# The first pair of heads: k transposed into two PSUM banks and copied in two halves, its rest first, and shorter first products of ones

## The chip, the cores and the metric

The kernel runs on one core of one Trainium2 chip. The metric is the device time of one execution in microseconds. Before the change it is 775.11 us, the median of three runs (774.7 to 775.67). Five engines work side by side: TensorE (PE, matmuls, with its weight loads shown as PEld), VectorE (DVE), ScalarE (ACT), GpSimd (POOL) and SyncE (SP, which issues most DMA transfers).

## The reference

Attention that keeps, for each query, only the scores not below the 32nd largest, followed by a feed-forward block with a squared ReLU:

```python
# q, k, v: (8, 8, 576, 64) float32 (batch, heads, sequence, head_dim)
scores = (1 / sqrt(64)) * q @ k^T
kth = the 32nd largest score of each row
scores = where(scores >= kth, scores, -1e9)
attn = softmax(scores)                       # over the row
x = (attn @ v), heads side by side           # (4608, 512)
h = maximum(x @ w_in, 0)                     # w_in (512, 2048)
out = (h * h) @ w_out                        # w_out (2048, 512), float32 out
```

## The kernel before

The work is cut into pairs of heads (four pairs for each of eight batches). Of each pair, q, k and v are loaded as rows (tiles rq, rk, rv), q and k are turned by PE into the tile qk (head dimension on the partitions), and v is copied to bf16 (vb). Queries are worked on in groups of 128 of both heads; the last 64 queries of two pairs together make a fifth group. For one group PE computes the scores of both heads into three PSUM banks (`score`), ACT copies them to SBUF (L755), DVE folds the 576 scores of each row into shorter lists of maxima (L905), POOL makes the lists of the minima (L900), and DVE finds the 32nd largest by rounds of MAX8 and MATCH_REPLACE8 (L934 to L946). ACT then makes a mask (L965), PE turns the scores and adds the mask in PSUM (`attend`), ACT takes the exponential (L1021), and PE multiplies by v. The results of two pairs are normalised, transposed, and fed to the feed-forward products (`feed`) in chunks of up to 256 rows.

No order of the instructions is written by hand. Every piece of work is recorded with `pl.op(engine, duration, priority, function, ...)`, with the tiles that it reads, writes, takes from a pool and releases. `Plan.schedule` (in the class Plan) then plays the whole program with these durations: each engine takes the ready piece with the lowest priority number whose tiles can be had. A piece with `nbf` isn't ready before that time from the start. A piece counts as ended after its duration plus a tail for its engine (TAIL: 0.165 us for PE, 0.12 for ACT, 0.084 for DVE) and 0.035 us, and only then is a tile's slot free. `Emitter` writes the engines' instructions in the order so found and puts in the semaphore waits, between instructions of one engine too. So a changed duration or piece anywhere can change the order of all that comes later.

PSUM has eight banks in three pools: `ps_s` (three banks, the scores), `ps_e` (three banks, the turned scores of `attend`), both with one slot that is handed out in the order in which the tiles were made, and `psum` (two single banks, for everything else, to whoever asks first).

For the first pair, three functions stand apart. `load_first` issues the transfers of rk (half from ACT's queue, which also loads its rest, the last 64 rows of both heads; half from SP's), of the first 128 rows of q (rq), and then of the other q rows (rq2). `first_pair` has PE transpose the first block of q into the tile tx (`o_x`), four blocks of k into the tile tk (`o_k`), and then the rest of k into columns 128 to 192 of tx. ACT copies q's 128 columns (L638) and the rest twice (L641) from tx, DVE copies k's 512 columns from tk in one instruction (L639). The score of group 0 needs all of these copies. The other blocks of q follow behind it (`later`).

PE has nothing to do until the first data lands. `setup` gives it products of a matrix of ones meanwhile, each of 512 columns into a tile of `psum` that nobody reads. They have the highest priority number (1e5) and are marked `fill`: such a piece is dropped when its turn comes more than 0.3 us after its `nbf`, and later ones also when PE has been busy enough. All wait for `lit`, the writing of the ones by DVE. The first ones have `nbf` 0, 0.43, 0.86 and so on up to 3.87 us and a duration of 0.43; later ones follow from 8 us on. In the profile all matmuls stand under the helpers' lines: L582 is `mm`, L585 is `tr`, a transpose.

## Time and profile before

| | |
|---|---|
| median of three runs | 775.11 us |
| the profiled execution | 774.41 us, its span 772.6 us |
| mean granted TensorE clock | 0.998 |
| instructions | 27813 |
| busy: PE, DVE, ACT, POOL | 713.3, 751.6, 717.9, 687.6 us |
| DMA | 52.63 MB, mean 68 GB/s |

The span runs from the first to the last instruction; what the execution takes beyond it lies around the program. A row of the timeline has the start, the duration, the engine, the line, the operation, the tile written and the tile read, the shapes, the count, and in brackets how long the engine had been idle before and what ended that. A row of a group has the count, then the busy time in total and the mean duration of one in ns, and then the idle time before them. The table of windows gives for each stretch the busy time of each engine with its number of instructions, the granted clock, the DMA engines' share and GB/s.

### The profile page before, as it was taken

The numbers are of one execution on the slowest core, as the hardware profiler recorded it, in microseconds if no ns is written. First come the engines' busy times: TensorE is split into PE (matmuls) and PEld (weight loads), VectorE is DVE, ScalarE is ACT, GpSimd is POOL, SyncE is SP. The second block draws the span as 40 slices with busy tenths as digits, with TensorE's granted clock in tenths as the row PEclk, the third lists the DMA queues.
The fourth block names the chain that finished last, engine by engine and source line by source line (L and its number), as shares of the span: only waits on it lengthen the run. The fifth ranks groups of instructions, "written<-read, shape, count | busy, mean of one in ns | idle before, by whom it ended". The sixth has DMA issues, their size and how long they took to land.

```text
span 772.6 us, 27813 instructions
## 1 busy us (share of the span) xinstructions
PE 713.3 (92%) x10680; PEld 528.2 (68%) x10680; DVE 751.6 (97%) x3589; ACT 717.9 (93%) x1141; POOL 687.6 (89%) x720
## 2 busy tenths in 40 slices
PE   7888888999989999998999889999899999999999
PEld 3656666666666676666767657686677777767776
DVE  5999999999999999999999999899999999999996
ACT  4799989899899999999999999999999999998884
POOL 4898998889789899989999899899999998989991
PEclk9999999999999999999999999999999999999999
DMA  7657452032400134103340043301332021100101
GB/s 191 182 137 196 132 135 52 23 83 48 114 11 9 51 83 95 32 16 85 70 99 10 18 111 86 69 6 46 93 82 67 11 68 38 34 23 23 36 23 34
DMA packets 145033, 52.63 MB, mean 68 GB/s; under 512 B 137088, under 2 KB 137344, under 8 KB 144896
## 3 DMA queue, kind: packets, MB, share of 16 engines
q1 hardware_dynamic: 144224, 50.66, 26.7%
q8 instruction: 84, 1.38, 0.8%
q14 instruction: 53, 0.43, 0.2%
q10 hardware_dynamic: 672, 0.16, 0.1%
HBM read 36.70 MB, written 9.44 MB: 60 GB/s over the span
## 4 chain that ended last, share of the span: by engine, by line
ACT 58%; PE 31%; DVE 8%; issue 2%; DVEq 0%; ACTq 0%
PE ps L582 26%; ACT w L965 13%; ACT p L1021 12%; ACT s L755 12%; ACT g L1140 7%; PE ps L585 5%; ACT hz L776 4%; ACT g L1155 3%; DVE f L943 2%; DVE f L905 2%; ACT o L1172 2%; DVE c L939 2%; ACT av L1087 2%; ACT qk L711 1%; ACT qk L712 1%
## 5 line engine op out<-in xcount | busy, mean ns | idle before, releaser
L900 POOL TENSOR_TENSOR f<-u,f 128x864 int32<-128x864 int32 x138 | 236.7, 1715 | 7.6
L965 ACT ACTIVATE w<-s,kth 128x576 bf16<-128x576 f32 x278 | 220.2, 829 | 3.5 <-DVE kth L946 3.5
L943 DVE MATCH_REPLACE8 f<-c,f 128x98 f32<-128x98 f32 (+2 forms) x840 | 221.2, 270 | 0.0
L939 DVE MAX8 c<-f 128x8 f32<-128x98 f32 (+2 forms) x840 | 201.5, 272 | 0.0
L582 PE MATMUL ps<-qk 64*128 64x384 f32 (+3 forms) x1280 | 179.5, 427 | 6.9 <-DVE f L905 5.8
L900 POOL TENSOR_TENSOR u<-f,s 128x576 int32<-128x576 int32 x138 | 166.5, 1206 | 16.6 <-DVE f L905 15.9
L1021 ACT ACTIVATE p<-ps 128x1152 bf16<-128x1152 f32 x144 | 169.1, 1174 | 12.5 <-PE ps L582 11.9
L755 ACT COPY s<-ps 128x1152 f32<-128x1152 f32 x140 | 162.0, 1157 | 17.3 <-PE ps L582 16.9
L582 PEld LDWEIGHTS ps<-qk 64*128 64x128 f32 (+1 forms) x1280 | 130.5, 175 | 39.6 <-DVE f L905 11.8
L582 PE MATMUL ps<-wo,g 128*128 128x512 bf16 (+1 forms) x592 | 142.9, 375 | 2.7 <-ACT qk L714 1.2
L582 PE MATMUL ps<-xt,win 128*128 128x256 bf16 (+1 forms) x1280 | 132.5, 252 | 8.5 <-ACT g L1140 3.6
L900 POOL TENSOR_TENSOR u<-s 128x288 int32<-128x288 int32 x138 | 110.2, 799 | 29.8 <-ACT s L755 26.5
L905 DVE TENSOR_TENSOR f<-ps,f 128x288 f32<-128x288 f32 x280 | 123.7, 442 | 0.1
L946 DVE MAX8 kth<-f 128x8 f32<-128x296 f32 x280 | 120.7, 456 | 0.0
L585 PEld LDWEIGHTS ps<-ident,s 64*128 64x128 f32 x2520 | 96.8, 139 | 30.9 <-ACT w L965 15.1
L582 PEld LDWEIGHTS ps<-xt,win 128*128 128x128 bf16 x1280 | 97.2, 98 | 29.3 <-ACT g L1140 6.0
L934 DVE MAX8 f<-f 128x8 f32<-128x288 f32 x280 | 114.7, 447 | 0.0
L585 PE MATMUL ps<-ident,s 64*128 64x64 f32 x2520 | 107.0, 227 | 4.6 <-ACT w L965 4.1
L1152 POOL TENSOR_TENSOR g<-g 128x512 bf16<-128x512 bf16 x86 | 89.4, 1042 | 2.9 <-ACT g L1140 2.6
L582 PEld LDWEIGHTS ps<-wo,g 128*128 128x128 bf16 x592 | 49.6, 98 | 55.2 <-issue 5.7
L1140 ACT ACTIVATE g<-ps 128x512 bf16<-128x512 f32 x140 | 86.2, 641 | 1.0 <-PE ps L582 0.9
L582 PEld LDWEIGHTS ps<-vb,p 128*128 128x128 bf16 (+1 forms) x1600 | 54.0, 100 | 32.7 <-ACT g L1140 10.5
(104 smaller groups left out, 859.1 us busy)
## 6 DMA issues: line engine op xcount, KB each, us to landing
rv<-in_v_dram SPq DMA_DIRECT2D x64, 128.0 KB, 2.4
rk<-in_k_dram SPq DMA_DIRECT2D x63, 128.0 KB, 2.5
rq<-in_q_dram SPq DMA_DIRECT2D x62, 128.0 KB, 2.5
out_dram<-o SPq DMA_DIRECT2D x31, 256.0 KB, 2.2
g<-in_moe_w_in_dram SPq DMA_DIRECT2D x8, 512.0 KB, 4.2
g<-in_moe_w_out_dram SPq DMA_DIRECT2D x8, 512.0 KB, 4.3
out_dram<-o SPq DMA_DIRECT2D x10, 128.0 KB, 2.3
rq<-in_q_dram SPq DMA_DIRECT2D x32, 32.0 KB, 2.5
```

The costliest lines, as they stand in the source:

```text
L582: return pe.matmul(o, l, r, start=start, stop=stop, skip_group_check=True)
L585: return pe.matmul(o, i, ident, is_transpose=True, skip_group_check=True, **kw)
L755: cp = [pl.op("act", 1.1, tg - LEAD + 1, lambda: act.copy(at(st)[:, :, 0:S], two(banks(ss)[:, FIRST_AT:], SECOND, S)), r=[ss], w=[st])]
L900: return pl.op("gp", dur, prio, lambda: gp.tensor_tensor(o().bitcast(I32), x().bitcast(I32), y().bitcast(I32), op), **kw)
L905: return dve(.36, lambda: vec.tensor_tensor(o(), two(banks(ss)[:, FIRST_AT + c:], SECOND, QUART), x(), ALU.max), r=[ss], **kw)
L934: prev[i] = [dve(.065 + HALF / 960, lambda i=i: vec.max(at(f)[:, i, A + 7:A - 1:-1], at(f)[:, i, M + QUART:E]), after=prev[i] + [low], hol ...
L939: lambda i=i, t=t, c0=c0, c1=c1: vec.max(eighth(t, i), at(f)[:, i, c0:c1]),
L943: lambda i=i, t=t, c0=c0, c1=c1: vec.match_replace(at(f)[:, i, c0:c1], eighth(t, i), at(f)[:, i, c0:c1], NEG), hold=[f])]
L946: ks.append(chain(kth, i, prev[i], .065 + (8 + HALF) / 960, lambda i=i: vec.max(eighth(kth, i), at(f)[:, i, A:M + QUART]), hold=[f]))
L965: masks[i:] = [pl.op("act", .77, tw + .8 * i, lambda i=i: act.activation(at(wt)[:, i, :], at(st)[:, i, 0:S], ACTF.Relu, bias=kth[:, i, n:n ...
L1021: return act.activation(at(pt)[:, :, :].rearrange("p c (h q) -> p h c q", h=2), bass.AP(x.tensor, x.offset, [x.ap[0], [APART, 2], [64, 9], ...
L1140: return act.activation(at(g)[:, 0:kf * nt], bank(hh)[:, 0:kf * nt], ACTF.Relu)
```

## The change

`first_pair` gets a fourth tile, tk2, from the pool `ps_e`. The rest of k is now transposed right after q's block (`o_r`) and ahead of the k blocks. Of these, blocks 0 and 1 go into tk and blocks 2 and 3 into tk2, and DVE copies each tile with an instruction of 256 columns. In `setup`, the list of the first products of ones keeps seven with a duration of 0.43 us; eleven with a duration of 0.11 us, 0.11 us apart from 3.01 us on, take the place of the other three, and a product with a duration under 0.2 us has 128 columns in place of 512.

```diff
         def first_pair(rq, rq2, rk, rv, qk, vb, base):
-            tk, tx, tq = Tile(psum), Tile(psum), Tile(psum)
+            tk, tx, tq, tk2 = Tile(psum), Tile(psum), Tile(psum), Tile(ps_e)
...
             o_x = pl.op("pe", .15, base - 45.2, flips(tx, rq, [0]), r=[rq], w=[tx], take=[tx, qk])
-            o_k = pl.op("pe", .5, base - 45.1, flips(tk, rk, [0, 1, 2, 3]), r=[rk], w=[tk], take=[tk], order=[o_x])
-            pl.op("pe", .2, base - 45, lambda: tr(bank(tx)[:, 128:192], at(rk)[0:64, 4, :, :].rearrange("p h d -> p (h d)"),
-                                                  ident32[0:64, 0:64]), r=[rk], w=[tx], order=[o_k])
+            o_r = pl.op("pe", .2, base - 45.15, lambda: tr(bank(tx)[:, 128:192], at(rk)[0:64, 4, :, :].rearrange("p h d -> p (h d)"),
+                                                  ident32[0:64, 0:64]), r=[rk], w=[tx], order=[o_x])
+            o_k = pl.op("pe", .25, base - 45.1, flips(tk, rk, [0, 1]), r=[rk], w=[tk], take=[tk], order=[o_r])
+            pl.op("pe", .25, base - 45, flips(tk2, rk, [2, 3]), r=[rk], w=[tk2], take=[tk2], order=[o_k])
             pl.op("act", .3, base - 42.5, lambda: act.copy(at(qk)[:, 0:128], bank(tx)[:, 0:128]), r=[tx], w=[qk])
-            pl.op("dve", .6, base - 42.5, lambda: vec.tensor_copy(at(qk)[:, 640:1152], bank(tk)), r=[tk], w=[qk])
+            for i, t in enumerate((tk, tk2)):
+                pl.op("dve", .3, base - 42.5 + .01 * i, lambda i=i, t=t: vec.tensor_copy(
+                    at(qk)[:, 640 + 256 * i:896 + 256 * i], bank(t)[:, 0:256]), r=[t], w=[qk])
...
-        times = [(COLD * i, COLD) for i in range(int(WARM / COLD)) if COLD * i < 4.2]
+        times = [(COLD * i, COLD) for i in range(7)] + [(3.01 + .11 * i, .11) for i in range(11)]
...
         for x, dur in times:
             t = Tile(psum)
-            pl.op("pe", dur, 1e5, lambda t=t: mm(bank(t), ones_bf[:, :], ones_bf[:, :].unsqueeze(1).broadcast_to(
-                [P, 4, P]), True), w=[t], take=[t], after=[lit], nbf=x, fill=True)
+            pl.op("pe", dur, 1e5, lambda t=t, n_=1 if dur < .2 else 4: mm(bank(t)[:, 0:P * n_], ones_bf[:, :], ones_bf[:, :].unsqueeze(1).broadcast_to(
+                [P, n_, P]), True), w=[t], take=[t], after=[lit], nbf=x, fill=True)
```

## The prediction

> **What bounds the kernel now.** I read the page's busy shares first, then a table of windows, then what VectorE (DVE) waits for, and last the timeline of the first 9 us, because everything that the diff names lies there.

> ```profile
> span 772.6 us, 27813 instructions
> PE 713.3 (92%) x10680; PEld 528.2 (68%) x10680; DVE 751.6 (97%) x3589; ACT 717.9 (93%) x1141; POOL 687.6 (89%) x720
> ```

> ```profile
> core 0: us, PE busy (x) PEld busy (x) DVE busy (x) ACT busy (x) POOL busy (x), PEclk, DMA share, GB/s
> 0.00:9.00 9.00, 7.20 (x30) 3.22 (x30) 0.96 (x3) 3.04 (x6) 6.16 (x43) 1.00 0.58 131
> 9.00:30.00 21.00, 17.04 (x150) 11.00 (x149) 20.74 (x92) 14.21 (x22) 9.94 (x12) 0.92 0.80 200
> 30.00:100.00 70.00, 58.94 (x932) 45.05 (x934) 69.93 (x337) 65.84 (x100) 65.33 (x59) 1.00 0.61 159
> 100.00:200.00 100.00, 92.45 (x1369) 65.82 (x1365) 99.75 (x481) 89.80 (x135) 88.45 (x78) 1.00 0.29 70
> 200.00:300.00 100.00, 92.10 (x1353) 68.51 (x1352) 99.14 (x476) 98.05 (x160) 91.28 (x98) 1.00 0.23 54
> 300.00:400.00 100.00, 91.93 (x1394) 67.56 (x1395) 99.71 (x476) 99.83 (x164) 93.37 (x100) 1.00 0.26 63
> 400.00:500.00 100.00, 93.67 (x1467) 70.06 (x1462) 97.48 (x467) 99.49 (x164) 92.35 (x101) 1.00 0.26 58
> 500.00:600.00 100.00, 94.78 (x1420) 72.18 (x1419) 98.75 (x473) 98.64 (x164) 94.44 (x100) 1.00 0.25 60
> 600.00:700.00 100.00, 95.97 (x1503) 72.61 (x1500) 99.58 (x485) 92.99 (x148) 89.99 (x83) 1.00 0.14 37
> 700.00:760.00 60.00, 58.12 (x967) 44.20 (x968) 58.96 (x290) 51.87 (x80) 55.74 (x52) 1.00 0.08 22
> 760.00:772.60 12.60, 11.06 (x122) 8.00 (x121) 6.60 (x24) 4.19 (x9) 0.52 (x1) 1.00 0.14 47
> ```

> ```profile
> DVE qk L639 <- PE ps L585: 4.6, 1, 4.6
> DVE f L905 <- ACT s L755: 3.5, 5, 2.6
> DVE f L943 <- POOL f L900: 2.8, 2, 1.9
> ```

> DVE is the bound. It loses 8.0 us in the first 9 us, 6.0 us in the last 12.6, and in the 751 us between only 7.0 us (0.26 + 0.07 + 0.25 + 0.86 + 0.29 + 2.52 + 1.25 + 0.42 + 1.04). So whatever the first pair gains or loses before DVE's first fold is passed on to the end nearly whole, and whatever a new order of the middle does is seen as a change of those 7.0 us. The waits (engine, line and releaser; then total, times, longest) say that 2.8 of the 7.0 come from two waits for POOL's fold.

> **The first 9 us.** These are rows of the timeline (start, duration, engine); some come from narrower windows, so that single instructions stand alone.

> ```profile
> 1.06 3.81 PE L582 MATMUL ps<-ones_bf 128*128 128x512 bf16 x10 [1.06 <-DVE ones_bf L1328]
> 1.27 0.49 SPq L609 DMA_DIRECT2D rq<-in_q_dram  x1
> 1.29 0.71 ACTq L609 DMA_DIRECT2D rk<-in_k_dram  x1
> 3.43 0.10 PEld L582 LDWEIGHTS ps<-ones_bf 128*128 128x128 bf16 x1 [0.32 <-PE ps L582]
> 3.86 0.10 PEld L582 LDWEIGHTS ps<-ones_bf 128*128 128x128 bf16 x1 [0.33 <-PE ps L582]
> 4.26 0.10 PEld L582 LDWEIGHTS ps<-ones_bf 128*128 128x128 bf16 x1 [0.30 <-PE ps L582]
> 4.48 0.10 PEld L582 LDWEIGHTS ps<-ones_bf 128*128 128x128 bf16 x1
> 4.49 0.38 PE L582 MATMUL ps<-ones_bf 128*128 128x512 bf16 x1
> 4.71 0.14 PEld L585 LDWEIGHTS ps<-ident,rq 128*128 128x128 f32 x1
> 4.93 0.86 PE L585 MATMUL ps<-ident,rk 128*128 128x128 f32 x5
> 5.21 0.14 PEld L585 LDWEIGHTS ps<-ident,rk 128*128 128x128 f32 x1
> 5.52 0.14 PEld L585 LDWEIGHTS ps<-ident,rk 64*128 64x128 f32 x1 [0.17 <-issue]
> 5.63 0.69 DVE L639 COPY qk<-ps 128x512 f32<-128x512 f32 x1 [4.62 <-PE ps L585]
> 5.83 0.27 ACT L638 COPY qk<-ps 128x128 f32<-128x128 f32 x1 [2.52 <-PE ps L585]
> 5.99 0.34 ACT L641 COPY qk<-ps 128x64 f32<-128x64 f32 x2
> 6.43 0.97 PEld L582 LDWEIGHTS ps<-qk 64*128 64x128 f32 x8 [0.78 <-ACT qk L641]
> 8.11 0.14 PEld L585 LDWEIGHTS ps<-ident,rq 64*128 64x128 f32 x1 [0.17 <-issue]
> 8.32 0.09 PEld L582 LDWEIGHTS ps<-ones_bf 128*128 128x128 bf16 x1
> ```

> The first score (6.43) waits for two chains that end together: DVE's copy of k (to 6.32) and ACT's three copies (to 6.33). The flips ahead of them are not held by data but by the products of ones, whose PSUM slots they take over. The last product runs from 4.49 to 4.87, and the first k flip, which takes its slot, comes 0.06 later at 4.93; the q flip at 4.71 takes the slot of the product before. The data was there, by these rows of the DMA view (KB, then us from issue to landing):

> ```profile
> rq<-in_q_dram SPq DMA_DIRECT2D x1, 64.0 KB, 2.8
> rk<-in_k_dram ACTq DMA_DIRECT2D x1, 32.0 KB, 3.3
> ```

> q landed at 1.27 + 2.8 = 4.07, the last of k at 1.29 + 3.3 = 4.59.

> **The change, part by part.** Durations of the nearest shapes:

> ```profile
> L582 PE MATMUL ps<-ident_bf 128*128 128x128 bf16 x81 | 7.5, 222 | 7.6 <-ACT p L1021 7.5
> L905 DVE TENSOR_TENSOR f<-ps,f 128x288 f32<-128x288 f32 x280 | 123.7, 442 | 0.1
> L918 DVE TENSOR_TENSOR f<-f,s 128x576 f32<-128x576 f32 x2 | 1.5, 748 | 0.0
> ```

> *Short products.* The first seven long ones stay, and 11 of 0.11 us replace the last three. By the planner's rules a short one holds one of two slots for 0.11 + 0.165 + 0.035 = 0.31 us, and a filler over 0.3 us late is dropped. Followed by hand: numbers 1, 4, 7 and 10 (from 0) are dropped and seven are issued, two per 0.31 us. On the chip the same two slots set the pace: each waits for the end of the product two before it. The first two shorts load at 3.86 and 4.26, where long ones 8 and 9 loaded, since they wait for the same products. From there two take 0.222 + 0.06 = 0.28 us, so numbers 4 and 6 load at about 4.54 and 4.82, and the sixth ends at 5.04. The q flip takes the sixth's slot: 5.10 in place of 4.71. Less is streamed, but the end comes 0.39 us later. The bounds are 4.65 if the flips wait for data alone (landing plus 0.06), and 5.28 if the shorts run at half clock (0.05 us more each).

> *Rest first.* The 64-row weight load doesn't overlap: 0.31 us after the last 128-row load (5.21 to 5.52), and the next 128-row load is 0.21 us behind it (8.11 to 8.32). So rest loads at 5.41, and the first k flip at 5.62. ACT's copies start when rest is done, at about 5.72, and take the same 0.50 us (5.83 to 6.33): 6.22. This chain is 0.11 us earlier than before and no longer ends last; its cover is 0.7 us of the DVE chain below.

> *Two copies.* From first k load to DVE's start is 0.70 us for four flips (4.93 to 5.63), 0.49 us for two at 0.105 us a flip. A copy of 256 columns, by the slope between 288 and 576 columns (1.06 ns a column), is 442 - 34 = 0.41 us, so two take 0.82 us, against 0.69 for one. The first copy starts at 5.62 + 0.49 = 6.11 and ends at 6.52; k's second half is ready at 6.32, so the second copy goes on to 6.93. Before, it was 6.32. The start is thus 0.61 us later. With the flips bound by data alone, rest at 4.65 gives copies from 5.35 to 6.17, a gain of 0.15 us; with the late bound of the shorts the loss is 0.8 us. I take +0.6, because the slot rule is seen twice in the rows (4.65 to 4.71, 4.87 to 4.93). The second bank itself costs nothing: it is taken from the pool of three banks that the first attention product uses only after the first top-k. The fourth PE instruction moves a dependence on POOL's set-up to the second score, where set-up has long ended.

> *The order of the rest.* The planner believes in another start than the chip: by its own durations the last copy is over at 6.46 before and 6.27 now (from its zero), so its first score is 0.19 us earlier. All later work is planned from there against release times that stay absolute (weights, fillers, the MoE products), with two PSUM slots in free order. I expect the written order of every engine to differ in many places. The work itself is the same, so DVE's busy time stays, and only the 7.0 us of gaps are drawn anew. How far they can move is read from the windows: 100 us lose between 0.25 and 2.52 us, mean 0.93, spread 0.86, so 7.5 such stretches spread by 2.4 us. The gaps can't fall below zero but can grow freely; I add 0.3 us for that.

> Sum: 774.41 (the profiled execution: 772.6 of span and 1.8 around it) + 0.6 + 0.3 = 775.3. The median of the three runs is 0.7 above that execution, so **776.0** on its scale. Bounds on the sum: start -0.15 to +0.8, order -2.8 (both POOL waits gone) to +4.8 (two standard spreads).

> [...] The weight loads of the ones are 0.43 apart up to 3.86, and 0.22 apart at 4.26 and 4.48: the array doubled its pace at about 4.2 (and the mean granted clock of 0.92 from 9 to 30 us says that it was lowered once more).

> [...]

> **Rivals.**
> 1. *Order worse, slower.* One more wait of DVE for POOL's fold at L943, or another stretch like 400 to 500 us. Price 2.5 us (that stretch's loss), total 775.1 + 0.6 + 2.5 = 778.2. For it: POOL is 89% busy, and ACT 98% to 99.8% from 200 to 600, so a fold planned late has little room to catch up. It decides from 1.0 us of added gaps.
> 2. *Order better, faster.* Both POOL waits go: -2.8 + 0.6, 772.9. Against it: such waits are rare already, and they must go without others coming.
> 3. *Cold start.* Half clock through the first score: four flips +0.3, the score's 0.97 us of loads and their products up to +1.2: 775.1 + 0.6 + 1.5 = 777.2. Against it: the first seven products are unchanged.
> 4. *Start as intended, order as good:* -0.15, 775.0.

> **How the numbers follow.** Forecast (start +0.6, gaps -1.0 to +2.0, so 774.7 to 777.7): 0.42. Rivals: 0.28, 0.20, 0.05, 0.05. About 0.2% (1.55 us) is what a measurement can tell from none; the three runs spread over 0.13%. Faster: rival 2 and a little, 0.21. Same: two thirds of the forecast and rival 4, 0.33. Slower: a third of the forecast, rivals 1 and 3, 0.46. The range leaves out the lower third of rival 2 and the upper third of rival 1: 772.0 to 780.5.

> **What would show it.** Seven long and seven short products, the q flip at about 5.1, two DVE copies of 0.41 us ending near 6.9, ACT's copies done 0.7 us earlier, first score near 7.0; DVE's busy time within 0.5 us of before plus 0.13; and the difference in total equal to the start's shift plus the change of DVE's gaps between 9 and 760 us. I am wrong if the shorts clear PE before 4.6 (the start is then earlier), if the order after 10 us is the same as before, or if the last 12 us change by over a microsecond, which nothing above prices.

## The result and the profile after

The changed kernel takes 777.39 us (median of ten runs, 776.48 to 779.47) against 775.34 us in the same runs of before. The ratio is 1.0026 with a 95% interval of 1.0016 to 1.0035, so it is slower by 2.0 us (1.2 to 2.7). The profiled execution took 777.31 us, 2.9 more than that of before.

From the page of the changed kernel, the span and the busy shares:

```profile
span 775.5 us, 27815 instructions
PE 712.7 (92%) x10680; PEld 528.6 (68%) x10680; DVE 751.9 (97%) x3590; ACT 718.3 (93%) x1141; POOL 688.1 (89%) x720
```

DVE is as busy as before to 0.3 us, so the time lies in what it waits for. The start, from the timeline of the changed kernel (all lines behind the first pair are 3 higher than before):

```profile
1.06 4.18 PE L582 MATMUL ps<-ones_bf 128*128 128x512 bf16 x14 [1.06 <-DVE ones_bf L1331]
5.21 0.14 PEld L585 LDWEIGHTS ps<-ident,rq 128*128 128x128 f32 x1
5.47 0.62 PEld L585 LDWEIGHTS ps<-ident,rk 64*128 64x128 f32 x5
5.95 0.33 ACT L644 COPY qk<-ps 128x64 f32<-128x64 f32 x2
6.16 0.76 DVE L641 COPY qk<-ps 128x256 f32<-128x256 f32 x2 [5.15 <-PE ps L585]
6.97 0.95 PEld L582 LDWEIGHTS ps<-qk 64*128 64x128 f32 x8 [0.87 <-DVE qk L641]
9.41 0.46 DVE L908 TENSOR_TENSOR f<-ps,s 128x288 f32<-128x288 f32 x1 [2.49 <-ACT s L758]
```

Fourteen products of ones hold PE until 5.24 us. The q flip comes at 5.21 (before: 4.71), DVE's two copies end at 6.92 (6.32), and the first score starts at 6.97 (6.43). DVE's first fold starts at 9.41. Before, it was this row:

```profile
8.90 0.46 DVE L905 TENSOR_TENSOR f<-ps,s 128x288 f32<-128x288 f32 x1 [2.58 <-ACT s L755]
```

So 0.51 of the 2.9 us is there at the first fold. Not all of it need be the change's: by the traces' records of the granted clock, the array has its full clock from 4.51 us in this execution and from 4.05 in that of before. Most of the rest is in DVE's waits. Behind the first fold and before 498 us, the changed kernel has these over 0.1 us (the wait stands in the brackets):

```profile
24.45 0.09 DVE L946 MATCH_VALUE_LOAD f<-c,f 128x8 f32 x1 [0.81 <-POOL f L903]
30.72 0.09 DVE L946 MATCH_VALUE_LOAD f<-c,f 128x8 f32 x1 [0.89 <-POOL f L903]
297.26 0.46 DVE L908 TENSOR_TENSOR f<-ps,s 128x288 f32<-128x288 f32 x1 [0.19 <-ACT s L758]
471.34 0.46 DVE L908 TENSOR_TENSOR f<-ps,s 128x288 f32<-128x288 f32 x1 [1.58 <-ACT s L758]
```

Before had these:

```profile
199.63 0.46 DVE L905 TENSOR_TENSOR f<-ps,s 128x288 f32<-128x288 f32 x1 [0.19 <-ACT s L755]
217.62 0.46 DVE L905 TENSOR_TENSOR f<-ps,s 128x288 f32<-128x288 f32 x1 [0.38 <-ACT s L755]
273.03 1.42 DVE L814 MAX8 hk<-hz 128x8 f32<-128x576 f32 x2 [0.43 <-POOL hz L812]
350.33 0.46 DVE L905 TENSOR_TENSOR f<-ps,s 128x288 f32<-128x288 f32 x1 [0.20 <-ACT s L755]
```

That is 3.47 us against 1.20. From 498 us on both kernels show the same waits with the same lengths, over 3 us later in the new one; the orders of DVE, ACT and POOL are the same again from 352 us on. The first of these waits, in the changed kernel and then in that before:

```profile
501.65 0.09 DVE L946 MATCH_VALUE_LOAD f<-c,f 128x8 f32 x1 [1.93 <-POOL f L903]
498.43 0.09 DVE L943 MATCH_VALUE_LOAD f<-c,f 128x8 f32 x1 [1.93 <-POOL f L900]
```

Start 0.51 and waits 2.27 make 2.78 us. These rows are 3.22 apart, so 0.44 us more lies in small waits and busy time that the lists leave out. DVE's last wait is 3.36 later, and the span ends 2.9 later: 0.46 us come back behind it.

The wait at 471 is of another kind than the two for POOL. Windows of the changed kernel around it (window, its length, busy time of PE, PEld, DVE, ACT and POOL with instructions, granted clock, DMA share, GB/s), and a row of PE's timeline of each kernel, the new one first:

```profile
463.00:464.00 1.00, 0.00 (x0) 0.00 (x0) 1.00 (x6) 1.00 (x5) 1.00 (x1) 1.00 0.67 153
465.00:466.00 1.00, 1.00 (x11) 0.78 (x8) 1.00 (x8) 0.98 (x3) 1.00 (x2) 0.66 0.86 196
467.00:468.00 1.00, 1.00 (x32) 1.00 (x28) 1.00 (x8) 0.17 (x1) 0.76 (x1) 0.50 0.10 15
```

```profile
464.32 0.36 PE L582 MATMUL ps<-vb,p 128*128 128x65 bf16 x6 [1.36 <-ACT qk L717]
```

```profile
462.55 0.62 PE L582 MATMUL ps<-vb,p 128*128 128x65 bf16 x14 [1.36 <-ACT qk L714]
```

PE idles 1.36 us in both kernels at this place. In the new kernel's execution the array then goes to half clock, ACT falls behind PE, and DVE waits 1.58 us; in the execution of before the clock stays full. ACT's and PE's instructions around it follow each other in the same order in both, so the written order at this place isn't what sets it.

Nor are these 1.58 us what parts the two kernels. A half-clock stretch of 3.41 us (465.31 to 468.72 here) takes 0.002 off the mean granted clock of an execution: half of 3.41 in 775.5 us. Five of the ten executions of the changed kernel stand at 0.998, one stretch, as in the profile of before; their median is 777.63 us. The five at 0.996, two stretches, as in this profile, have 777.38. The tally above is of one execution.

### The profile page after: what moved, and what is told of

Read it like the earlier page. It is cut to its first block, busy times and chain, and to the rows that moved or that the text cites. A ratio compares the mean times of both kernels' runs of the same rounds, so it can differ in the third digit from the quotient of the medians.

```text
span 775.5 us, 27815 instructions
## 1 busy us (share of the span) xinstructions
PE 712.7 (92%) x10680; PEld 528.6 (68%) x10680; DVE 751.9 (97%) x3590; ACT 718.3 (93%) x1141; POOL 688.1 (89%) x720
## 4 chain that ended last, share of the span: by engine, by line
ACT 53%; PE 26%; DVE 16%; POOL 2%; issue 2%; POOLq 0%; ACTq 0%
PE ps L582 22%; ACT w L968 12%; ACT p L1024 11%; ACT s L758 11%; ACT g L1143 6%; DVE f L946 5%; PE ps L585 5%; DVE f L908 4%; DVE c L942 3%; ACT hz L779 3%; ACT g L1158 2%; DVE f L937 2%; DVE kth L949 2%; ACT qk L714 1%; ACT av L1090 1%
## 5 line engine op out<-in xcount | busy, mean ns | idle before, releaser
L582 PE MATMUL ps<-qk 64*128 64x384 f32 (+3 forms) x1280 | 179.8, 428 | 9.7 <-DVE f L908 7.9
L582 PEld LDWEIGHTS ps<-qk 64*128 64x128 f32 (+1 forms) x1280 | 130.9, 175 | 41.0 <-DVE f L908 13.0
L582 PE MATMUL ps<-wo,g 128*128 128x512 bf16 (+1 forms) x592 | 142.9, 375 | 2.1 <-ACT av L1090 1.1
L582 PE MATMUL ps<-xt,win 128*128 128x256 bf16 (+1 forms) x1280 | 132.7, 253 | 6.4 <-ACT av L1090 2.7
L585 PEld LDWEIGHTS ps<-ident,s 64*128 64x128 f32 x2520 | 97.2, 139 | 34.5 <-ACT w L968 19.8
L582 PEld LDWEIGHTS ps<-xt,win 128*128 128x128 bf16 x1280 | 97.7, 98 | 27.1 <-issue 6.7
L585 PE MATMUL ps<-ident,s 64*128 64x64 f32 x2520 | 107.6, 227 | 6.0 <-ACT w L968 5.6
L582 PEld LDWEIGHTS ps<-wo,g 128*128 128x128 bf16 x592 | 49.6, 98 | 53.7 <-issue 5.7
L582 PEld LDWEIGHTS ps<-vb,p 128*128 128x128 bf16 (+1 forms) x1600 | 53.9, 100 | 34.0 <-ACT g L1143 10.4
```

The lines of the kernel that those rows point to most:

```text
L582: return pe.matmul(o, l, r, start=start, stop=stop, skip_group_check=True)
L585: return pe.matmul(o, i, ident, is_transpose=True, skip_group_check=True, **kw)
```

## Experiments

**Start and order apart.** My theory was a sum: a start later by half a microsecond, and waits that the new order puts into the middle. The rivals: the late start is the whole cause, or the half-clock stretch is. The planner's order behind the first pair hangs on one thing that the change touches, the planned time at which the first score can start. So each half can be had alone by setting planned durations, which change no instruction.

The new start with the old order: all of the change, and in the plan

```diff
-            pl.op("act", .3, base - 42.5, lambda: act.copy(at(qk)[:, 0:128], bank(tx)[:, 0:128]), r=[tx], w=[qk])
-            for i, t in enumerate((tk, tk2)):
-                pl.op("dve", .3, base - 42.5 + .01 * i, lambda i=i, t=t: vec.tensor_copy(
+            pl.op("act", .8, base - 42.5, lambda: act.copy(at(qk)[:, 0:128], bank(tx)[:, 0:128]), r=[tx], w=[qk])
+            for i, t, d_ in ((0, tk, .55), (1, tk2, .1)):
+                pl.op("dve", d_, base - 42.5 + .01 * i, lambda i=i, t=t: vec.tensor_copy(
```

> The changed kernel's first pair and short products, with the planner's durations of the first copies set so that the planner starts the first score when it did before: every engine's later order is that of before. Theory 1 (the time is the sum of a later start and of gaps that the new order puts into the middle): first score near 6.97 us, DVE's first fold near 9.4, no wait of DVE for POOL's fold before 100 us, +0.5 us on before (ratio 1.0007). Theory 2 (the later start is the whole cause, the order harmless): +2.0 us (1.0026), with new waits of DVE between 9 and 100 us. Theory 3 (the half-clock stretch near 465 us is the cause): +0.5 us or +2, according to whether a second such stretch falls into a run, with no system.

Every engine's order behind the first pair was that of before. Rows of its timeline:

```profile
5.32 0.14 PEld L585 LDWEIGHTS ps<-ident,rq 128*128 128x128 f32 x1
9.59 0.46 DVE L905 TENSOR_TENSOR f<-ps,s 128x288 f32<-128x288 f32 x1 [2.58 <-ACT s L755]
200.80 0.46 DVE L905 TENSOR_TENSOR f<-ps,s 128x288 f32<-128x288 f32 x1 [0.19 <-ACT s L755]
```

Ratio 1.0018 (1.0008 to 1.0028): +1.4 us (0.6 to 2.2). The first fold is 0.69 us late, and the next wait of over 0.1 us is the one that before has at 199.63. It comes 1.17 later, so another half microsecond came behind the first fold, without a wait of over 0.1 us. No wait for POOL's fold comes before 100 us. That excludes theory 2 as to the waits: a late start doesn't make them. The size lies above my 0.5; the 0.69 of the rows is just inside the interval.

The old start with the new order: the kernel before, and in the plan

```diff
-            pl.op("act", .3, base - 42.5, lambda: act.copy(at(qk)[:, 0:128], bank(tx)[:, 0:128]), r=[tx], w=[qk])
-            pl.op("dve", .6, base - 42.5, lambda: vec.tensor_copy(at(qk)[:, 640:1152], bank(tk)), r=[tk], w=[qk])
+            pl.op("act", .2, base - 42.5, lambda: act.copy(at(qk)[:, 0:128], bank(tx)[:, 0:128]), r=[tx], w=[qk])
+            pl.op("dve", .55, base - 42.5, lambda: vec.tensor_copy(at(qk)[:, 640:1152], bank(tk)), r=[tk], w=[qk])
             for i, c in enumerate((576, 1152)):
-                pl.op("act", .25, base - 42.4 + .1 * i, lambda c=c: act.copy(
+                pl.op("act", .2, base - 42.4 + .1 * i, lambda c=c: act.copy(
```

> The first pair and the long products of before, with the planner's durations of the first copies set so that the planner starts the first score when it does in the changed kernel: every engine's later order is that of the changed kernel. Theory 1: first score at 6.43 us, two waits of DVE for POOL's fold near 24 and 30 us of 0.8 to 0.9 us each, +1.0 to +1.7 us on before (1.0013 to 1.0022). Theory 2: 0 (1.0000). Theory 3: as likely 0 as +1.6, by the clock stretch alone.

```profile
8.85 0.46 DVE L905 TENSOR_TENSOR f<-ps,s 128x288 f32<-128x288 f32 x1 [2.57 <-ACT s L755]
23.91 0.09 DVE L943 MATCH_VALUE_LOAD f<-c,f 128x8 f32 x1 [0.83 <-POOL f L900]
30.13 0.09 DVE L943 MATCH_VALUE_LOAD f<-c,f 128x8 f32 x1 [0.89 <-POOL f L900]
563.72 0.46 DVE L905 TENSOR_TENSOR f<-ps,s 128x288 f32<-128x288 f32 x1 [0.96 <-ACT s L755]
570.36 0.46 DVE L905 TENSOR_TENSOR f<-ps,s 128x288 f32<-128x288 f32 x1 [0.47 <-ACT s L755]
```

Ratio 1.0016 (1.0007 to 1.0025): +1.2 us (0.5 to 1.9), as theory 1 expected. The first fold is where it was, and both waits for POOL are there, 0.83 and 0.89 us long. There is no wait at 471; instead two of 0.96 and 0.47 us stand behind a half-clock stretch that starts at 560.35 us in this execution. So the two waits for POOL go with the order. They aren't the whole of its price in this profile: their 1.72 us stand in place of the 1.20 of before, 0.52 more, and the half-clock waits of 1.43 us make most of the rest of the 1.95 by which it is longer.

The half-clock stretch of the middle starts at 465.31 us in the changed kernel's profile and at 560.35 in this one, but such stretches aren't without system. Two or more of them (a mean granted clock of 0.996 or less) came in 13 of the 21 executions with the new order, the changed kernel's among them, and in 15 of 186 with the old order, whatever their start. So the order brings them more often; by which of its gaps isn't shown. What they cost in the mean isn't settled either: the three executions of this run with one stretch took 775.85 to 776.35 us, the eight with two 776.36 to 777.35, but in the changed kernel the two groups don't differ.

What the new order does at 17 us, in rows of ACT, then POOL, of the kernel before:

```profile
16.76 1.12 ACT L755 COPY s<-ps 128x1152 f32<-128x1152 f32 x1 [1.88 <-PE ps L582]
17.77 1.44 ACT L965 ACTIVATE w<-s,kth 128x576 bf16<-128x576 f32 x2
17.96 0.80 POOL L900 TENSOR_TENSOR u<-s 128x288 int32<-128x288 int32 x1 [2.88 <-ACT s L755]
21.41 1.71 POOL L900 TENSOR_TENSOR f<-u,f 128x864 int32<-128x864 int32 x1
```

and of the old start with the new order:

```profile
17.23 0.77 ACT L965 ACTIVATE w<-s,kth 128x576 bf16<-128x576 f32 x1 [2.35 <-DVE kth L946]
17.91 1.10 ACT L755 COPY s<-ps 128x1152 f32<-128x1152 f32 x1
19.10 0.80 POOL L900 TENSOR_TENSOR u<-s 128x288 int32<-128x288 int32 x1 [3.90 <-ACT s L755]
22.08 1.71 POOL L900 TENSOR_TENSOR f<-u,f 128x864 int32<-128x864 int32 x1
```

Before, ACT copies the scores first and then makes both masks of the group ahead. In the new order one mask stands ahead of the copy, and that mask needs DVE's result. The copy starts 1.15 us later, POOL's first fold 1.14 later, its last one ends at 23.79 in place of 23.12, and DVE, which comes to it at 23.08, waits 0.83.

**The parts of the start.** The short products alone, and the new first pair alone, each with the old order by planned durations as above, each twice:

> Only the first products of the changed kernel (seven of 512 columns, then seven of 128), the first pair and every later order as before. If the flips are held by the slots of the products: q flip at 5.21 us, k flips at 5.30, DVE's copy to 6.69, first score near 6.80, +0.37 us (1.0005). If the short products cost nothing and the new first pair makes the later start: first score at 6.43, 0.

> The short products alone once more, for a narrower interval beside the burst: +0.4 us (1.0005) if the later start of the rows is all, +1.0 us or more (1.0013) if thin products cost beyond it, by a later full clock.

> Only the new first pair (rest first, two banks, two copies), the ten long products and every later order as before. By the trace of the changed kernel DVE's second copy ends 1.71 us after the q flip's weight load: 4.71 + 1.71 = 6.42, first score near 6.47, +0.04 us. By the prediction's own steps (0.31 and 0.21 us of weight loads that don't overlap, two copies of 0.41): copies to 6.54, first score 6.65, +0.2. If the pair does what its parts suggest (half the copy on the path): earlier by 0.1 to 0.2.

> The new first pair alone once more, for a narrower interval: +0.04 to +0.2 us (1.0001 to 1.0003) by the steps of the prediction, below 0 if halving the copy helps.

The diffs are the two halves of the change. The shorts gave 1.0017 (1.0002 to 1.0031) and 1.0008 (0.9995 to 1.0020); the pair 1.0005 (0.9995 to 1.0014) and 1.0006 (0.9997 to 1.0015). None of the four shows a gain, and only the first interval excludes zero. The profiles tell more. The q flip behind the paced shorts, in the first run:

```profile
5.33 0.18 PEld L585 LDWEIGHTS ps<-ident,rq 128*128 128x128 f32 x1
```

In the second it comes at 5.01. The clock differs between the two. In the second the loads are 0.28 us apart from 3.86 to 4.14, so full clock came before 4.14, and the first score starts at 6.62, against 6.43 in the profile of before. In the first the array is at half clock to beyond 5 us, and the score starts at 7.09; the run with the old pair, ten long products and a late clock that is shown below has it at 7.07. So in these rows the shorts cost about 0.2 us where full clock comes early, and nothing where it comes late.

The pair alone, second run:

```profile
4.71 0.10 PEld L582 LDWEIGHTS ps<-ones_bf 128*128 128x128 bf16 x1 [0.32 <-PE ps L582]
5.14 0.18 PEld L585 LDWEIGHTS ps<-ident,rq 128*128 128x128 f32 x1 [0.32 <-PE ps L582]
6.42 0.76 DVE L639 COPY qk<-ps 128x256 f32<-128x256 f32 x2 [5.42 <-PE ps L585]
7.29 0.98 PEld L582 LDWEIGHTS ps<-qk 64*128 64x128 f32 x8 [0.93 <-ACT qk L641]
```

Here ten long products stand ahead, as before, but the q flip comes at 5.14 and not at 4.71: the loads are still 0.43 us apart at 4.71 and 5.14, so the array got its full clock about a microsecond later than in the profile of before. The first run of the pair caught it later still: full clock from 6.95 us by its record, the first score at 7.64, the first fold at 10.11, and the longest of its ten times, 777.18 us. I had not allowed for this. The prediction's start was read from one execution with an early full clock. A fairer comparison needs one with a late clock and the old pair; a run below (planner's cost 0.35) has it, with the q flip at 5.14 too:

```profile
6.26 0.69 DVE L639 COPY qk<-ps 128x512 f32<-128x512 f32 x1 [5.26 <-PE ps L585]
7.07 0.97 PEld L582 LDWEIGHTS ps<-qk 64*128 64x128 f32 x8 [0.78 <-ACT qk L641]
```

From the same q flip the new pair ends its copies at 7.18 against 6.95, and the score starts 0.22 later, near what the steps said (0.2). Some of it may be clock: the q flip's own matmul takes 0.42 us in the pair's run and 0.38 in the other, so full clock came a little later in the pair's.

**Is it the slots?** The shorts as one piece in one slot, so that none waits for another:

```diff
-        times = [(COLD * i, COLD) for i in range(int(WARM / COLD)) if COLD * i < 4.2]
+        times = [(COLD * i, COLD) for i in range(8)]
...
-            pl.op("pe", dur, 1e5, lambda t=t: mm(bank(t), ones_bf[:, :], ones_bf[:, :].unsqueeze(1).broadcast_to(
-                [P, 4, P]), True), w=[t], take=[t], after=[lit], nbf=x, fill=True)
+            pl.op("pe", dur, 1e5, lambda t=t, k_=7 if 3 < x < 3.1 else 1, n_=1 if 3 < x < 3.1 else 4: [
+                mm(bank(t)[:, 0:P * n_], ones_bf[:, :], ones_bf[:, :].unsqueeze(1).broadcast_to([P, n_, P]), True)
+                for _ in range(k_)][-1], w=[t], take=[t], after=[lit], nbf=x, fill=True)
```

> Seven products of 512 columns and seven of 128 as in the changed kernel, but the seven thin ones are one piece in one PSUM slot, so none waits for another; first pair and later order as before. If the slots' waits make the short products late: the thin ones stream behind the seventh long one in 0.4 us at full clock (0.75 at half), q flip near 4.7 us (5.05 at half clock), k flips no later than before, time -0.3 to +0.2 us on before (0.9996 to 1.0003). If thin products are late in themselves: q flip near 5.2 again and +0.4 us or more.

```profile
4.67 0.17 PEld L585 LDWEIGHTS ps<-ident,rq 128*128 128x128 f32 x1
4.97 0.42 PEld L585 LDWEIGHTS ps<-ident,rk 128*128 128x128 f32 x4
6.47 0.97 PEld L582 LDWEIGHTS ps<-qk 64*128 64x128 f32 x8 [0.78 <-ACT qk L641]
```

The same fourteen products let the q flip go at 4.67 in place of 5.01 to 5.33, and the first score at 6.47 in place of 6.62 and 7.09. An earlier clock doesn't explain it: the burst's thin products are still 0.11 us apart up to 4.66, where those of the second run of the shorts were at full clock before 4.14. The pace of the two slots is what made the shorts late. Behind the q flip the gain shrinks: the first k flip goes at 4.97, against 5.08 in that run. In time the run can't tell: 1.0008 (0.9996 to 1.0021).

**A late start alone, and fewer products.** The kernel before with four more long products (the tenth piece issues five), and with eight in place of ten. The first diff is of the one, the second of the other:

```diff
-            pl.op("pe", dur, 1e5, lambda t=t: mm(bank(t), ones_bf[:, :], ones_bf[:, :].unsqueeze(1).broadcast_to(
-                [P, 4, P]), True), w=[t], take=[t], after=[lit], nbf=x, fill=True)
+            pl.op("pe", dur, 1e5, lambda t=t, k_=5 if 3.8 < x < 3.9 else 1: [mm(
+                bank(t), ones_bf[:, :], ones_bf[:, :].unsqueeze(1).broadcast_to([P, 4, P]), True)
+                for _ in range(k_)][-1], w=[t], take=[t], after=[lit], nbf=x, fill=True)
```

```diff
-        times = [(COLD * i, COLD) for i in range(int(WARM / COLD)) if COLD * i < 4.2]
+        times = [(COLD * i, COLD) for i in range(8)]
```

> The kernel before with 14 first products of 512 columns in place of ten, at the planner's old cost, so that every later order is as before: a later start alone, with the array as busy as before. First score later by 4 x 0.215 = 0.86 us, near 7.3. If a late start is passed on 1:1 (theory 1): +0.9 us (1.0011). If a late start is paid about twice, as the 0.69 us of the new start with the old order seemed to be in its median: +1.7 us (1.0022). If the chip's middle absorbs it: 0.

> The kernel before with eight first products of 512 columns in place of ten, every later order as before. If the flips were held by the products' slots alone: k flips at 4.65 us (the last of k lands at 4.59) in place of 4.93, first score near 6.15, -0.28 us (0.9996). If the flips were held by data after all: first score at 6.43, 0. If fewer products leave the array at half clock: first score later than 6.43, slower by 0.3 us or more.

The late start gave 1.0020 (1.0011 to 1.0030), +1.6 us. Its profiled execution has the first fold here:

```profile
10.49 0.46 DVE L905 TENSOR_TENSOR f<-ps,s 128x288 f32<-128x288 f32 x1 [2.58 <-ACT s L755]
```

That is 1.59 us behind 8.90, and not the 0.86 that four products at full clock take: in this execution, too, the full clock came late (from 5.57 us by its record). Behind the first fold of the run with planner's cost 0.35, which had a late clock as well (9.53), it is 0.96. At 201.55 this execution is 1.92 us behind the wait that before has at 199.63, so between the two profiles a late start is passed on whole, and a little is added. Whether the times pay it once or twice stays open: in the profiles with the same ten first products the full clock came between 3.98 and 6.95 us. If that holds for the executions of before that were not profiled, the four products should add about 0.9 in the mean, an estimate. That is the lower end of the interval (0.9 to 2.3), and the +1.7 expected for "twice" lies nearer its middle.

Eight products gave 0.9999 (0.9989 to 1.0009): the 0.28 us that I hoped for, if there, can't be seen. The profile has the first k flip at 4.71 and the first score at 6.34, 0.09 earlier than before although full clock came only at 5.01. Then a half-clock stretch from 66.45 to 69.86 us costs this execution more than that. DVE's instructions, in the order of before, are 0.1 us early until 68 us and 0.8 late at 77, with these waits between:

```profile
69.53 0.46 DVE L905 TENSOR_TENSOR f<-ps,s 128x288 f32<-128x288 f32 x1 [0.28 <-ACT s L755]
75.24 0.46 DVE L905 TENSOR_TENSOR f<-ps,s 128x288 f32<-128x288 f32 x1 [0.42 <-ACT s L755]
```

**Other orders.** To see how the order draws, three more kernels with the first pair's instructions of before; only the planned cost of ACT's first copy is 0.2, 0.35 or 0.4 in place of 0.3, for instance:

```diff
-            pl.op("act", .3, base - 42.5, lambda: act.copy(at(qk)[:, 0:128], bank(tx)[:, 0:128]), r=[tx], w=[qk])
+            pl.op("act", .35, base - 42.5, lambda: act.copy(at(qk)[:, 0:128], bank(tx)[:, 0:128]), r=[tx], w=[qk])
```

> The kernel before in every instruction of the first pair; only the planner's cost of ACT's first copy is 0.2 in place of 0.3, so that it starts the first score 0.1 us earlier and orders the rest anew. First score at 6.43. If an order drawn anew costs by chance: between -2.5 and +4 us, read as other waits of DVE between 9 and 500 us. If the planner's order is indifferent: 0.

> The kernel before in every instruction of the first pair, with the planner's cost of ACT's first copy at 0.35 in place of 0.3: a third order drawn anew. If an order costs by chance: between -2.5 and +6 us, with other waits of DVE between 9 and 500 us than before. If the planner's order is indifferent: 0.

> As the run before it, with the planner's cost of ACT's first copy at 0.4 in place of 0.3, so that the planner starts the first score later and orders the rest anew, another way. First score at 6.43. If an order drawn anew costs by chance: between -2.5 and +4 us. If the planner's order is indifferent: 0.

| planned cost | ratio (95% interval) | us |
|---|---|---|
| 0.20 | 1.0007 (0.9996 to 1.0017) | +0.5 |
| 0.30 (before) | 1 | 0 |
| 0.35 | 0.9991 (0.9982 to 1.0000) | -0.7 |
| 0.40 (four executions) | 1.0057 (1.0038 to 1.0076) | +4.4 |

The last one also moves the later q flips ahead of the first score, which costs it part of a microsecond at the start. Its profile then shows more waits of both kinds: for POOL (the longest of the new ones 0.71 us, at 435.96), and this one, behind a half-clock stretch from 467.00 us:

```profile
475.08 0.46 DVE L905 TENSOR_TENSOR f<-ps,s 128x288 f32<-128x288 f32 x1 [1.57 <-ACT s L755]
```

So 0.05 to 0.1 us in one planned duration gave times from -0.7 to +4.4 us; only the last is clear of zero, and it is twice what the whole change costs. The order at 0.35 may be a little faster than before; its interval ends at 1.0000, and I don't call it faster.

## Why the prediction was right or wrong

The forecast was 776.0 us, in a range of 772.0 to 780.5 with slower as the likeliest sign; it came out at 777.39. The sum added 0.9 us and the times say 2.0 (1.2 to 2.7), so the sign was right, the sum was low, and the width of the range, taken from the gaps of the order, held the result.

- *Short products.* Right, with the pace as the reason: seven long and seven short, the q flip predicted at 5.10 and found at 5.21, and the burst shows that the slots set it. It held where full clock came before the fill ended, as here (4.51 against 5.24 us); in the execution where it came later, the shorts cost nothing (first score at 7.09 against 7.07).
- *Rest first, two copies.* Right in sum: the copies were predicted to end at 6.93 and end at 6.92, ACT's chain at 6.22 and at 6.28. That the sum fits so well is luck, for two errors offset each other. The flips start 0.1 later, and the second copy overlaps the first by 0.07 (0.76 for both, not 0.82).
- *Start passed on.* "I take +0.6" was near the rows (first score +0.54, first fold +0.51) and low for the times: the new start alone cost 1.4 (0.6 to 2.2). Both ends of this are loose. The rows compare two executions with different clocks. With the old start, the first fold is at 8.85, 8.90, 9.22 and 9.53 us in four profiles, with full clock from 3.98, 4.05 and 4.76 us by the record and from about 5.4 by the rows; with the new start it is at 9.41 and 9.59, with full clock from 4.51 and 5.13. At the same clock the new start is thus 0.2 to 0.3 us late, an estimate from these rows. So the reading of the start from one execution is a sample, and the rows explain less of the 1.4 than it seems. Half a microsecond more shows in the profile of the new start with the old order, between the first fold (0.69 late) and 200 us (1.17). Where the rest comes from stays open. Whether thin products also delay the full clock can't be settled from these runs; the parts' first runs (1.3 and 0.4) add up to 1.7 and their second ones (0.6 and 0.5) to 1.1, around 1.4, but with wide intervals.
- *The order of the rest.* The term was mis-sized: I added 0.3 us, and the new order alone cost 1.2 (0.5 to 1.9). The mechanism that the runs show is in part the one of the first rival, waits of DVE for POOL's fold, at a smaller price (0.81 and 0.89 in place of 2.5), and most of that is offset by waits of before that are gone. The other part, half-clock stretches that came more often with the new order (two or more in 13 of 21 executions, against 15 of 186), the prediction did not have. The spread of 2.4 us that I read from the windows was about right: four orders drawn anew gave +1.2, +0.5, -0.7 and +4.4 (the last with a later start in it), which spread by 2.2.
- *The clock.* I gave the third rival, half clock through the first score, a chance of 0.05 by the rows of one execution, in which the loads of the ones double their pace at about 4.2 us. The time of the first full clock varied: with ten long products it came from 4.05 us in the profile of before and from 6.95 in the first run of the pair alone. In that run all flips ran at half clock, and the first score came at 7.64, so a part of the third rival's case came about with the long products too. And half clock came where I did not look, at 465.31 us, with 1.58 us of waiting in that execution; the sum had no term for it.
- "I am wrong if ... the last 12 us change by over a microsecond": they didn't. The last waits are the same to 0.01 us.

## What to carry to other kernels

Fillers that take turns in a few buffers were paced here by the round trip of a buffer, not by their own size: in two slots the last four short products load two per 0.29 us (from 4.63 and 4.92 us, and then the q flip at 5.21). Made smaller without more buffers, they let PE go at 5.24 us in place of 4.87, with the array at full clock from 4.51. In one piece and one buffer the same products ended at 4.91 us, in place of 5.01 to 5.38. In a kernel whose order a planner writes, compare a change with its own order held fixed: a planned duration changed by 0.05 to 0.1 us gave -0.7 to +4.4 us here, and a local edit of half a microsecond can't be judged beneath that. A start that depends on the array's clock (full here from 3.98 to 6.95 us with the same first products) should be read from several executions before it is priced, and two starts compared at the same clock. Where the order is held, the same instruction in two traces gives the shift at every point, which says more than a list of waits.
